# Attention and Mish block on one core: reciprocals of the first row block issued right behind kv's masks, and two weight jobs of w2 started earlier

## The chip, the cores and the metric

The kernel runs on one core of one Trainium2 chip. The core has a matrix engine (TensorE, PE in the profile, with its weight loads as PEld), a vector engine (VectorE, DVE), a scalar engine for activations (ScalarE, ACT), a general engine (GpSimd, POOL) and an engine that here only issues transfers (SyncE, SP). Each engine works through its own queue in order and waits on semaphores for the others; transfers are issued from the SP and POOL queues. The metric is the time of one execution on the device in microseconds (us). Before the change it is 505.05 us, the median of 3 runs (504.99 to 505.3).

## The reference

2,048 rows of width 512 pass through an attention part and a two-layer part, each with a layer norm, whose scale, shift and gate come from a condition vector `c`:

```python
mod = (_silu(c) @ w_mod).reshape(c.shape[0], 6, 1, -1)      # sa, ca, ga, sb, cb, gb
h = _layernorm(x) * (1 + ca) + sa
x = x + ga * A(h, A_wqkv, A_wo)
h = _layernorm(x) * (1 + cb) + sb
x = x + gb * B(h, B_w1, B_b1, B_w2)

# A: linear attention, 32 heads of width 16, phi(t) = where(t > 0, t + 1, exp(t)) + 1e-6
kv  = einsum("bhsd,bhse->bhde", phi(k), v)
z   = einsum("bhsd->bhd", phi(k))
num = einsum("bhqd,bhde->bhqe", phi(q), kv)
den = einsum("bhqd,bhd->bhq", phi(q), z)[..., None] + 1e-6
A   = (num / den) @ wo

# B: 512 -> 1792 -> 512
h = x @ w1 + b1
B = (h * tanh(softplus(h))) @ w2
```

## The kernel before, in words

**Tiling.** The rows are cut into 4 blocks of 512 (b = 0 to 3), each into 4 tiles of 128 (t). Matrix products keep nearly full float32 accuracy by splitting each operand into a high half, made by ACT as a copy, and a low half, made by DVE as the difference (`split`, line 71); `mm3` (line 65) then issues three matmuls, high by high, low by high and high by low (lines 67, 68, 69). Tiles of 128 x 512 in SBUF come from one pool of 101 places (`sb`), PSUM has three groups of buffers: `acc` (4), `h` (3) and `tp` (1).

**Order of work.** The program fixes the order by hand. Matmuls stand in the main flow; what follows a product on the other engines is written as a generator that is spawned and then moved on by one step at each `tick()`, in the order of spawning. So a `yield` means "the rest is issued one tick later", and each engine's queue has the order in which the ticks issue its instructions.

**Stages.** Keys and their sums come first, block by block. Then (from line 724) query units run, each giving one 128 x 512 piece of q, which ACT and DVE turn into phi(q) (lines 241 to 244). Between them stand the small products that make `kv` (line 746; two instructions of DVE, line 749, mask it to its 16 x 16 blocks) and from it m = kv @ wo (line 758). Every query unit's buffer is one of the three in `h`.

**The denominators** of a block are made by `attend(b, wait, queue)` (line 593). Its first step issues 32 small matmuls (line 598) into the buffer `tp`. Its second adds a small number (line 602), takes reciprocals (line 603), writes them to DRAM through `queue` (line 605) and reads them back as four tiles `rd`, spread over the heads' columns (line 609). After `wait` yields, counted from the end of that second step, the phi(q) tiles are multiplied by `rd` (line 617), two per tick, and split into halves `qs`. These are the operands of `o_unit(b, t)`, which makes the attention's output for one tile of rows; `o_post` (line 629) adds it to the input x, which empties the buffer. For blocks 0 to 2 `queue` is POOL, for block 3 it is SP.

**Around kv**: query unit (1,0), the early rows of w1 (`early_rows`), the first step of `attend(0, 4)`, the kv products, the masks, and then query units (1,1) to (1,3), each with a tick. The denominators' second step is issued in the tick behind unit (1,1), behind what was spawned earlier: modulation dot products (line 165) and the phi of unit (1,0).

**The output loop** (line 780) goes over units n = 4b + t for b = 1 to 3. Beside `o_unit` it transposes the normalised rows of blocks 0 and 1 for the second part (line 696), and at n = 5 spawns `attend(3, 3, sp)`. At n = 11 and 12 it spawns `w2_job(0)` and `w2_job(1)`. A `w2_job(f)` (line 499) asks for 128 rows of w2 on the SP queue (line 501), waits two ticks, multiplies them by the gate gb (line 504), one tick later makes the high half, one tick later the low half, and a tick after that issues two writes of these halves to DRAM on the POOL queue (line 510), from where later blocks reload them. Block 0 uses the halves directly in `d_unit`. The loop ends at n = 14; the last two output units stand among the first products of the second part, which uses a Strassen-like scheme with seven products (lines 836 to 860).

Of the kernel before, what the change touches and what calls it, by code (L numbers as in the profile page):

```python
# [13 lines left out]
P = 128  # L14
# [11 lines left out]
def block_kernel(ctx: ExitStack, tc: tile.TileContext, x, wqkv, wo, w1, b1t, w2, c, wmodt, out):  # L26
    nc = tc.nc
    act, dve, pool, pe, sp = nc.scalar, nc.vector, nc.gpsimd, nc.tensor, nc.sync
# [9 lines left out]
    def sb(name, dt=F32, shape=(P, 512)):  # L38

        return big.tile(list(shape), dt, tag="T", name=name, bufs=SLOTS)  # L40

    def ps(tag, name, shape=(P, 512)):
        return psp.tile(list(shape), F32, tag=tag, name=name, bufs=PBUFS[tag])
# [6 lines left out]
    def spawn(gen):  # L50
        fresh.append(gen)

    def tick():

        running.extend(fresh)
        fresh.clear()
        for g in list(running):
            if next(g, "end") == "end":
                running.remove(g)

    def run(gen):
        for _ in gen:
            pass
# [7 lines left out]
    def split(name, t, keep, key, lo_engine=dve, hi_engine=act):  # L71

        hi, lo = sb(f"{name}h", F32R, t.shape), sb(f"{name}l", F32R, t.shape)
        if hi_engine is act:
            act.activation(hi, t, AF.Copy)
        else:
            hi_engine.tensor_copy(hi, t)
        if lo_engine is dve:
            yield
        lo_engine.tensor_tensor(lo, t, f32(hi), op=ALU.subtract)  # L80
        keep[key] = hi, lo
# [4 lines left out]
    def load_x(b, j, key="x", eng=sp):  # L86
        t = xt[key, b, j] = sb(f"{key}_{b}_{j}")
        r0 = 512 * b + P * j
        eng.dma_start(t, x[r0:r0 + P, :])
# [84 lines left out]
    def ln_stats(key, b, j, t):  # L174

        for d, name, shape in (mv, "mv", [P, 4, 2]), (rs, "rs", [P, 4]), (nb, "nb", [P, 4]):
            if (key, b) not in d:
                d[key, b] = cst.tile(shape, F32, tag=name, name=f"{name}_{key}_{b}", bufs=NB)
        st6 = cst.tile([P, 6], F32, tag="st6", name=f"st6_{key}_{b}_{j}", bufs=4)
        dve.bn_stats(st6, t)  # L180
        dve.bn_aggr(mv[key, b][:, j, :], st6)

    def ln_eps(key, b, lo=0, hi=4):
        dve.tensor_scalar(rs[key, b][:, lo:hi], mv[key, b][:, lo:hi, 1], EPS, 1.0, op0=ALU.add, op1=ALU.mult)  # L184

    def ln_rstd(key, b, lo=0, hi=4):

        y = rs[key, b][:, lo:hi]
        pool.tensor_tensor(y, y, half[:, lo:hi], op=ALU.pow)  # L189

    def ln_shift(key, b, lo=0, hi=4):

        dve.scalar_tensor_tensor(nb[key, b][:, lo:hi], mv[key, b][:, lo:hi, 0], -1.0, rs[key, b][:, lo:hi],  # L193
                                 op0=ALU.mult, op1=ALU.mult)

    def ln_apply(key, b, j, t, dst, engine):
        if engine is act:
            act.activation(dst, t, AF.Identity, bias=nb[key, b][:, j:j + 1], scale=rs[key, b][:, j:j + 1])  # L198
        else:
            engine.tensor_scalar(dst, t, mv[key, b][:, j, 0:1], rs[key, b][:, j:j + 1],  # L200
                                 op0=ALU.subtract, op1=ALU.mult)

    def act_sums(key, b, t, v):

        if (key, b) not in rs:
            for d, name in (rs, "rs"), (nb, "nb"):
                d[key, b] = cst.tile([P, 4], F32, tag=name, name=f"{name}_{key}_{b}", bufs=NB)
        scrap = sb(f"scrap_{key}_{b}_{t}")
        sums = cst.tile([P, 2], F32, tag="sums", name=f"sums_{key}_{b}_{t}", bufs=6)
        act.activation(scrap, v, AF.Identity, scale=-1.0 / D, accum_out=sums[:, 0:1])  # L210
        act.activation(scrap, v, AF.Square, bias=sums[:, 0:1], accum_out=sums[:, 1:2])
        return sums

    def sums_eps(key, b, t, sums):
        dve.tensor_scalar(rs[key, b][:, t:t + 1], sums[:, 1:2], 1.0 / D, EPS, op0=ALU.mult, op1=ALU.add)  # L215
        ln_rstd(key, b, t, t + 1)

    def sums_shift(key, b, t, sums):
        dve.tensor_tensor(nb[key, b][:, t:t + 1], sums[:, 0:1], rs[key, b][:, t:t + 1], op=ALU.mult)  # L219
# [64 lines left out]
    def q_unit(b, g):  # L284
        p = ps("h", f"pq_{b}_{g}")
        gs = slice(P * g, P * (g + 1))
        for k in range(4):
            mm3(p, [w[:, gs] for w in wq[k]], hT["x", b, k], k == 0, k == 3)
        pq[b, g] = sb(f"q_{b}_{g}")
        spawn(phi(p, f"q_{b}_{g}", pq[b, g]))  # L290
# [205 lines left out]

    w2s, w2d, op_a = {}, {}, {}

    def w2_job(f, wait=2):
        t = sb(f"w2r_{f}")  # L500
        sp.dma_start(t, w2[P * f:P * (f + 1), :])
        for _ in range(wait):
            yield
        dve.tensor_tensor(t, t, bc["gb"], op=ALU.mult)
        yield
        yield from split(f"w2_{f}", t, w2s, f)
        yield
        for i in range(2):
            w2d[f, i] = drp.tile([P, D], F32R, name=f"w2d_{f}_{i}")
            pool.dma_start(w2d[f, i], w2s[f][i])  # L510
# [82 lines left out]
    def attend(b, wait, queue=pool):  # L593

        p = ps("tp", f"den_{b}")[:, 0:P]
        for g in range(4):
            for t in range(4):
                pe.matmul(p[32 * t:32 * (t + 1), :], hmask[:, g, :], pq[b, g][:, P * t:P * (t + 1)],
                          start=g == 0, stop=g == 3)
        yield  # L600
        rden = cst.tile([P, P], F32, tag="rden", name=f"rden_{b}", bufs=2)
        dve.tensor_scalar(rden, p, TINY, 1.0, op0=ALU.add, op1=ALU.mult)
        dve.reciprocal(rden, rden)  # L603
        d = drp.tile([32, 512], F32, name=f"rden_d_{b}")
        queue.dma_start(bass.AP(tensor=d.tensor, offset=d.offset, ap=[[P, 4], [512, 32], [1, P]]), rden)  # L605
        rd = []
        for g in range(4):
            r = sb(f"rd_{b}_{g}")
            queue.dma_start(r, bass.AP(tensor=d.tensor, offset=d.offset + 8 * g * 512,
                                     ap=[[512, 8], [0, 16], [1, 512]]))  # L610
            rd.append(r)
        for _ in range(wait):
            yield
        parts = []
        for g in range(4):
            t = pq[b, g]
            dve.tensor_tensor(t, t, rd[g], op=ALU.mult)  # L617
            parts.append(split(f"qs_{b}_{g}", t, qs, (b, g)))
            next(parts[-1])
            if g % 2:  # L620
                yield
                run(parts.pop(0))
                run(parts.pop(0))
# [32 lines left out]
    def norm_each(b, t):  # L656

        if t < 2:
            yield
            sums = act_sums("n", b, t, xt["r", b, t])  # L660
            yield
            sums_eps("n", b, t, sums)
            yield
            sums_shift("n", b, t, sums)
        else:
            ln_stats("n", b, t, xt["r", b, t])
            ln_eps("n", b, t, t + 1)
            ln_rstd("n", b, t, t + 1)
            yield
            ln_shift("n", b, t, t + 1)  # L670
        v = xt["n", b, t] = sb(f"n_{b}_{t}")
        ln_apply("n", b, t, xt["r", b, t], v, act)
# [62 lines left out]
    tick()  # L735
    run(early_rows[0])
    next(early_rows[1])
    attending = attend(0, 4)
    next(attending)
    spawn(attending)  # L740
    kv_ps = ps("acc", "kv_ps")
    for g in range(4):
        for k in range(4):
# [3 lines left out]
    for j in range(2):  # L747
        js = slice(64 * j, 64 * (j + 1))
        dve.tensor_tensor(kv.rearrange("p (g m) -> p g m", g=4)[js, :, js],
                          kv_ps.rearrange("p (g m) -> p g m", g=4)[js, :, js],  # L750
                          bmask[js, js].unsqueeze(1).to_broadcast([64, 4, 64]), op=ALU.mult)
    for g in range(1, 4):
        q_unit(1, g)
        load_x(2, g, "r")
        tick()
# [24 lines left out]
    for b in range(1, NB):  # L780
        for t in range(4):
            n = 4 * b + t
            for i, j in order.get(n, ()):
                transpose_f(i, j, "h")
                spawn(split_b(i, j, f"b{j // 2 + 1}{i + 1}"))
            if n in (12, 13):
                spawn(columns(0, n - 12, ("b11", "b12", "b21", "b22")))
            if n == 14:
                break
            o_unit(b, t)  # L790
            if b == 1:
                spawn(norm_each(1, t))
            if n == 5:
                spawn(attend(3, 3, sp))
            if n in (11, 12):
                spawn(w2_job(n - 11))
            tick()


# [185 lines left out]
```

## Time and profile before

| | us |
|---|---|
| median of 3 runs | 505.05 |
| the profiled execution, as a whole | 506.47 |
| its span, from its first to its last instruction | 504.7 |
| PE busy in the span | 495.5 |
| DVE busy | 360.3 |
| ACT busy | 257.8 |
| POOL busy | 112.9 |
| PE clock granted | 1.00 of full speed |

A row of a timeline has the start in us from the span's start, the length in us, the engine, the line of the program, the operation, the tile written, the tiles read, their shapes and a count; in brackets stands how long the engine had been idle before it and what ended that idle time. Successive rows of one engine can overlap, since an instruction starts while the one before it drains; the distance from start to start is what an instruction costs its queue. A row of the chain of waits has a start, a length and what filled it; the chain is followed back from the last instruction, at each step to what released it. In a row by windows each engine's busy time stands with its number of instructions, and behind them the granted clock, the busy share of the 16 transfer engines and the GB/s that they moved.

### The profile page before, as it was taken

Reading aid. Unit: us, or ns where it says so; the run is one execution under the profiler, and the core shown is the slowest. Engines: PE = TensorE matmul, PEld = TensorE weight load, DVE = VectorE, ACT = ScalarE, POOL = GpSimd, SP = SyncE. Lnnn points to the kernel's source line nnn. Section 1 sums busy time; section 2 is a strip of 40 time slices with the busy share of each in tenths; the row PEclk is TensorE's granted clock in tenths of the full one; section 3 lists DMA queues with packets and bytes.
Section 4 is the critical chain, followed back from the end, with each engine's and each line's share of the span. In section 5 each row is a group of like instructions: output and inputs, shape, how many; then the busy total and the mean of one; then the engine's idle time right before and its main releaser. Section 6 shows DMA issues by size and latency. Waiting matters only on the chain.

```text
span 504.7 us, 6900 instructions
## 1 busy us (share of the span) xinstructions
PE 495.5 (98%) x2396; PEld 404.9 (80%) x2396; DVE 360.3 (71%) x707; ACT 257.8 (51%) x463; POOL 112.9 (22%) x204
## 2 busy tenths in 40 slices
PE   7999999999999999999999999999999999999996
PEld 5778888878778888878888888888888888888885
DVE  6889785889987978986987785359886556745302
ACT  6767573523351987836677765357253344445000
POOL 3480000100212311210233345421210111470000
PEclk9999999999999999999999999999999999999999
DMA  8821503472553315372565499982842445597002
GB/s 282 303 83 44 166 21 105 153 244 72 137 111 92 88 33 161 125 228 66 157 197 188 145 297 260 348 240 87 249 130 59 125 126 155 157 338 236 32 1 83
DMA packets 52233, 77.29 MB, mean 153 GB/s; under 512 B 5805, under 2 KB 20277, under 8 KB 52198
## 3 DMA queue, kind: packets, MB, share of 16 engines
q0 software_dynamic: 19600, 37.45, 25.6%
q1 hardware_dynamic: 32452, 39.14, 24.6%
q8 instruction: 19, 0.31, 0.2%
q10 hardware_dynamic: 146, 0.26, 0.1%
q14 instruction: 16, 0.13, 0.1%
HBM read 60.83 MB, written 15.99 MB: 152 GB/s over the span
## 4 chain that ended last, share of the span: by engine, by line
PE 84%; DVE 9%; DMA 4%; issue 1%; ACT 1%; POOL 1%; DVEq 0%; POOLq 0%; ACTq 0%
PE oacc L69 10%; PE oacc L67 10%; PE oacc L68 10%; PE p_s L67 5%; PE p_s L69 5%; PE p_s L68 5%; PE p_a L67 3%; PE p_a L69 3%; PE p_a L68 3%; DMA rd<-rden_d 3%; PE gacc L68 3%; PE gacc L69 3%; PE gacc L67 3%; PE pk L69 2%; PE pk L68 2%; PE pk L67 2%
## 5 line engine op out<-in xcount | busy, mean ns | idle before, releaser
L516 POOL DMA_DIRECT2D w2b<-w2d x84 | 44.9, 538 | 102.3 <-PE p_a L69 27.0
L827 ACT ACTIVATE ub<-c,b1c 128x512 f32<-128x512 f32 x28 | 19.0, 718 | 57.5 <-DVE c L836 53.8
L836 DVE TENSOR_TENSOR u<-p_s,u 128x512 f32<-128x512 f32 x28 | 19.4, 692 | 35.2 <-PE p_s L69 25.5
L819 DVE TENSOR_TENSOR rb<-oacc,rb 128x512 f32<-128x512 f32 x8 | 5.5, 692 | 32.9 <-PE oacc L69 32.9
L836 DVE TENSOR_TENSOR u<-p_a,u 128x512 f32<-128x512 f32 x26 | 17.6, 689 | 7.5 <-PE p_a L69 6.9
L698 ACT ACTIVATE hf_n<-tp_n,mc 128x512 f32<-128x512 f32 x16 | 11.7, 771 | 19.5 <-PE tp_n L696 19.5
L189 POOL TENSOR_TENSOR rs_n<-rs_n,half 128x1 f32<-128x1 f32 x16 | 9.4, 589 | 53.9 <-DVE rs_n L215 44.3
L804 ACT ACTIVATE u<-u,b1c 128x512 f32<-128x512 f32 x26 | 18.5, 712 | 2.6 <-DVE u L836 2.6
L836 DVE TENSOR_TENSOR c<-p_s,u 128x512 f32<-128x512 f32 x28 | 18.0, 683 | 1.9 <-PE p_s L69 1.3
L241 ACT ACTIVATE e_q<-pq 128x512 f32<-128x512 f32 x16 | 9.3, 588 | 18.4 <-PE pq L69 18.4
L853 ACT ACTIVATE u<-p_a 128x512 f32<-128x512 f32 x12 | 7.1, 588 | 18.7 <-PE p_a L69 18.7
L241 ACT ACTIVATE e_k<-pk 128x512 f32<-128x512 f32 x16 | 9.4, 591 | 13.3 <-PE pk L69 13.1
L617 DVE TENSOR_TENSOR q<-q,rd 128x512 f32<-128x512 f32 x16 | 10.7, 689 | 6.9 <-DMA rd<-rden_d 6.8
L189 POOL TENSOR_TENSOR rs_x<-rs_x,half 128x1 f32<-128x1 f32 (+1 forms) x10 | 7.1, 716 | 32.1 <-DVE rs_x L184 31.3
L243 DVE TENSOR_SCALAR e_k<-e_k 128x512 f32<-128x512 f32 x16 | 6.9, 430 | 10.0 <-ACT e_k L241 9.9
L198 ACT ACTIVATE x<-x,nb_x,rs_x 128x512 f32<-128x512 f32 x15 | 11.6, 808 | 4.7 <-DVE nb_x L193 3.5
L605 POOL DMA_DIRECT2D rden_d<-rden x3 | 2.2, 738 | 45.7 <-DVE rden L603 45.7
L198 ACT ACTIVATE r<-r,nb_n,rs_n 128x512 f32<-128x512 f32 x8 | 6.5, 809 | 10.1 <-DVE nb_n L219 9.3
L244 DVE SCALAR_TENSOR_TENSOR q<-pq,e_q 128x512 f32<-128x512 f32 x16 | 11.1, 692 | 0.7
L244 DVE SCALAR_TENSOR_TENSOR ku<-pk,e_k 128x512 f32<-128x512 f32 x16 | 11.1, 692 | 0.7
L629 DVE TENSOR_TENSOR r<-o,r 128x512 f32<-128x512 f32 x16 | 10.8, 680 | 0.4 <-PE o L69 0.4
L180 DVE BATCH_NORM_STATS2 st_x<-x 128x6 f32<-128x512 f32 x13 | 8.9, 682 | 2.9 <-DMA x<-in_x_dram 2.9
(1118 smaller groups left out, 1751.9 us busy)
## 6 DMA issues: line engine op xcount, KB each, us to landing
w2b<-w2d POOLq DMA_DIRECT2D x84, 256.0 KB, 5.1
w1p<-in_w_dram SPq DMA_DIRECT2D x28, 256.0 KB, 3.1
wm<-in_wmodt_dram SPq DMA_DIRECT2D x24, 256.0 KB, 5.7
r<-in_x_dram SPq DMA_DIRECT2D x16, 256.0 KB, 2.4
x<-in_x_dram SPq DMA_DIRECT2D x15, 256.0 KB, 5.5
w2r<-in_w_dram SPq DMA_DIRECT2D x14, 256.0 KB, 3.4
rd<-rden_d POOLq DMA_DIRECT2D x12, 256.0 KB, 5.7
wr<-in_wqkv_dram SPq DMA_DIRECT2D x8, 256.0 KB, 3.2
```

The source lines that it names most:

```text
L67: pe.matmul(o, st[0], mv[0], start=start, stop=False)
L68: pe.matmul(o, st[0], mv[1], start=False, stop=False)
L69: pe.matmul(o, st[1], mv[0], start=False, stop=stop)
L189: pool.tensor_tensor(y, y, half[:, lo:hi], op=ALU.pow)
L198: act.activation(dst, t, AF.Identity, bias=nb[key, b][:, j:j + 1], scale=rs[key, b][:, j:j + 1])
L241: act.activation(e, p, AF.Exp)
L244: dve.scalar_tensor_tensor(dst, p, 0.0, e, op0=ALU.max, op1=ALU.add)
L516: pool.dma_start(w2s[f][i], w2d[f, i])
L698: act.activation(hf[b, j], p, AF.Identity, bias=mc[:, 12 + j:13 + j], scale=mc[:, 16 + j:17 + j])
L804: act.activation(u, p, AF.Mish, bias=b1c[:, f:f + 1])
L827: act.activation(u, p, AF.Mish, bias=b1c[:, f:f + 1])
L836: dve.tensor_tensor(out, p, u, op=ALU.add)
```

## The change

Two places are touched.

First, around kv. The generator for block 0's denominators is now advanced by hand through its second step directly behind the two masks of kv, and only then spawned. Since this step ends at the first of its waiting yields, one of them is used up at that place, and `wait` is 5 in place of 4.

Second, the first two jobs of w2. Asking for the rows becomes a function of its own, `load_w2`, which is called for f = 0 and 1 at n = 4; `w2_job` then finds them asked for and starts with the multiplication, without waiting. Both jobs are spawned at n = 7 instead of n = 11 and 12. The other twelve jobs are as before.

```diff
+    w2r = {}
+
+    def load_w2(f):
+        w2r[f] = sb(f"w2r_{f}")
+        sp.dma_start(w2r[f], w2[P * f:P * (f + 1), :])
+
     def w2_job(f, wait=2):
-        t = sb(f"w2r_{f}")
-        sp.dma_start(t, w2[P * f:P * (f + 1), :])
-        for _ in range(wait):
-            yield
+        if f not in w2r:
+            load_w2(f)
+            for _ in range(wait):
+                yield
+        t = w2r[f]
         dve.tensor_tensor(t, t, bc["gb"], op=ALU.mult)
...
-    attending = attend(0, 4)
+    attending = attend(0, 5)
     next(attending)
-    spawn(attending)
     kv_ps = ps("acc", "kv_ps")
...
                           bmask[js, js].unsqueeze(1).to_broadcast([64, 4, 64]), op=ALU.mult)
+    next(attending)
+    spawn(attending)
     for g in range(1, 4):
...
+            if n == 4:
+                load_w2(0)
+                load_w2(1)
             if n == 5:
                 spawn(attend(3, 3, sp))
-            if n in (11, 12):
-                spawn(w2_job(n - 11))
+            if n == 7:
+                spawn(w2_job(0))
+                spawn(w2_job(1))
             tick()
```

## The prediction

> **What bounds the kernel now.** I read the page first (shares, chain of waits), then the list of PE's waits, then TensorE's timeline around each wait, and last the chain that leads into it.
>
> ```profile
> span 504.7 us, 6900 instructions
> ...
> PE 495.5 (98%) x2396; PEld 404.9 (80%) x2396; DVE 360.3 (71%) x707; ACT 257.8 (51%) x463; POOL 112.9 (22%) x204
> ...
> PE 84%; DVE 9%; DMA 4%; issue 1%; ACT 1%; POOL 1%; DVEq 0%; POOLq 0%; ACTq 0%
> ```
>
> TensorE (PE) is busy 98% of the span, so only the few places where it stands still can be won. PE's own list of waits from 105 to 240 us (waiter, releaser, us in all, times, longest) has two entries:
>
> ```profile
> PE p_s L67 <- DVE r L629: 0.7, 1, 0.7
> PE o L69 <- DVE qs_2l L80: 0.4, 1, 0.4
> ```
>
> The timeline (start, length, engine, line) shows a third, shorter one, and prices them from start to start:
>
> ```profile
> 145.45 0.39 PE L69 MATMUL pq<-hT_x_3h,wq_3l 128*128 128x512 f32 x1
> 145.98 0.50 PE L67 MATMUL pq<-hT_x_0h,wq_0h 128*128 128x512 f32 x1
> 146.32 0.40 PE L68 MATMUL pq<-hT_x_0l,wq_0h 128*128 128x512 f32 x1
> ...
> 150.19 0.39 PE L67 MATMUL o<-m_2h,qs_2h 128*128 128x512 f32 x1
> 150.42 0.39 PE L68 MATMUL o<-m_2l,qs_2h 128*128 128x512 f32 x1
> 151.25 0.50 PE L69 MATMUL o<-m_2h,qs_2l 128*128 128x512 f32 x1 [0.44 <-DVE qs_2l L80]
> 151.59 0.39 PE L67 MATMUL o<-m_3h,qs_3h 128*128 128x512 f32 x1
> ...
> 218.12 0.39 PE L69 MATMUL p_s<-t_1h,s_0l 128*128 128x512 f32 x1
> 219.23 0.50 PE L67 MATMUL p_s<-t_0h,s_0h 128*128 128x512 f32 x1 [0.73 <-DVE r L629]
> 219.57 0.39 PE L68 MATMUL p_s<-t_0l,s_0h 128*128 128x512 f32 x1
> ```
>
> The undisturbed step is 0.23 (150.19 to 150.42). **Stall 1** (last query unit of block 2, waiting for a PSUM buffer): 145.98 - 145.45 - 0.23 = 0.30, and the step after it is 0.34, 0.11 more than usual: 0.41. **Stall 2** (first output unit, waiting for qs_2l): 0.83 - 0.23 = 0.60, plus 0.11: 0.71. **Stall 3** (third Strassen product, waiting for the buffer of output unit (3,0), which DVE empties late): 1.11 - 0.23 = 0.88, plus 0.11: 0.99. Together 2.11 us, all that this change can win directly.
>
> **Part A: the reciprocals of block 0.** Rows of DVE, POOL and PE, in order of time:
>
> ```profile
> 125.62 0.69 DVE L165 SCALAR_TENSOR_TENSOR wm<-wm,sc_row 128x512 f32<-128x512 f32 x1
> ...
> 127.30 0.69 DVE L244 SCALAR_TENSOR_TENSOR q<-pq,e_q 128x512 f32<-128x512 f32 x1
> ...
> 127.91 0.28 DVE L602 TENSOR_SCALAR rden<-den 128x128 f32<-128x128 f32 x1
> ...
> 128.23 0.95 DVE L603 RECIPROCAL rden<-rden 128x128 f32<-128x128 f32 x1
> ...
> 129.47 0.76 POOL L605 DMA_DIRECT2D rden_d<-rden  x1 [36.25 <-DVE rden L603]
> ...
> 129.97 0.39 PE L67 MATMUL pq<-hT_x_0h,wq_0h 128*128 128x512 f32 x1
> ...
> 132.70 2.38 POOL L609 DMA_DIRECT2D rd<-rden_d  x4 [2.48 <-PE pq L69]
> ...
> 140.68 0.69 DVE L617 TENSOR_TENSOR q<-q,rd 128x512 f32<-128x512 f32 x1 [2.12 <-DMA rd<-rden_d]
> 141.71 0.69 DVE L617 TENSOR_TENSOR q<-q,rd 128x512 f32<-128x512 f32 x1 [0.34 <-DMA rd<-rden_d]
> ...
> 145.24 0.69 DVE L244 SCALAR_TENSOR_TENSOR q<-pq,e_q 128x512 f32<-128x512 f32 x1
> ...
> 150.57 0.63 DVE L80 TENSOR_TENSOR qs_2l<-q,qs_2h 128x512 fp32r<-128x512 f32 x1
> ```
>
> No instruction is added. L602 and L603 move to where the first modulation dot product stands, right behind the masks: 127.91 - 125.62 = 2.29 us earlier. The write to DRAM and the four row reads follow them in POOL's queue, which had idled 36.25 us, so they move by 2.29 too. The count of yields goes from 4 to 5 because one is used up before the spawn; the products (L617) stay in their tick, so only their wait for data shrinks: 140.68 becomes 138.39, 141.71 becomes 139.42.
>
> What is pushed back: the two instructions (0.28 + 0.95 = 1.23 us) go ahead of two modulations and of the phi of query unit (1,0), whose last instruction ends 1.23 later, at 129.22. It frees the buffer for the unit that PE begins at 129.97; 0.75 us are left, so this costs nothing (if the cover were gone, at most 1.23 on PE). From 129.2 on DVE's queue is as before.
>
> What follows the products on DVE runs back to back up to qs_2l, so it comes earlier by what the products gain. Stall 1 was released by the instruction at 145.24: now 142.95, done 143.64, wanted at 145.68. Stall 2 by qs_2l: 150.57 + 0.63 - 2.29 = 148.91, wanted at 150.65 - 0.41 = 150.24. Both vanish as soon as the rows land 0.95 us earlier. The bounds for that landing are 0 (the transfer engines finish everything at the old time; 8 us passed between the first request and the first product) and above 2.29 (the requests now go out before SP's loads of that moment, not after). I take 2.29, since both steps behind the reciprocals waited for nothing but their predecessor. **Part A: -1.12**, between 0 and -1.12.
>
> **Part B: the rows of w2's first two jobs.** Rows of SP, of the chain of waits (start, length), of DVE, PE and ACT, and one window (the last three numbers: granted clock, share of the 16 transfer engines, GB/s):
>
> ```profile
> 183.09 0.69 SPq L605 DMA_DIRECT2D rden_d<-rden  x1
> ...
> 188.60 0.82 SPq L501 DMA_DIRECT2D w2r<-in_w_dram  x2
> ```
>
> ```profile
> 187.86 8.04 DMA rd<-rden_d
> ...
> 204.55 0.60 DVE w2r L504
> ...
> 210.67 0.69 DVE w2r L504
> ...
> 212.56 0.60 DVE w_0l L80
> ...
> 216.17 0.60 DVE w_1l L80
> ...
> 218.58 0.61 DVE r L629
> ```
>
> ```profile
> 189.74 0.69 DVE L617 TENSOR_TENSOR q<-q,rd 128x512 f32<-128x512 f32 x1 [0.56 <-DMA rd<-rden_d]
> 191.49 0.69 DVE L617 TENSOR_TENSOR q<-q,rd 128x512 f32<-128x512 f32 x1 [1.06 <-DMA rd<-rden_d]
> ...
> 197.73 0.68 DVE L80 TENSOR_TENSOR qs_2l<-q,qs_2h 128x512 fp32r<-128x512 f32 x1
> ```
>
> ```profile
> 200.62 0.39 PE L69 MATMUL o<-m_2h,qs_2l 128*128 128x512 f32 x1
> ```
>
> ```profile
> 192.22 0.63 ACT L75 ACTIVATE qs_1h<-q 128x512 fp32r<-128x512 f32 x1 [0.83 <-DVE q L617]
> ```
>
> ```profile
> 192.00:194.00 2.00, 2.00 (x13) 1.70 (x12) 2.00 (x5) 1.78 (x4) 0.00 (x0) 1.00 1.02 226
> ```
>
> Loads: two requests (0.82 us of SP) move from behind block 3's row reads to before its reciprocals' write. SP's next work is that write at 183.09, so they pass no one who is ready; and 2 x 256 KB no longer share the engines with the row reads that end the chain at 195.90 (187.86 + 8.04). A late tile buffer would hold that write; the before kernel bounds this only loosely, as w2r went out at 188.60, before its own unit.
>
> DVE: four instructions of about 0.60 each, 2.40 us, leave the unbroken DVE run that ends with the release of stall 3 at 218.58. The two multiplications land in unit 7, just ahead of the idle 0.56 and 1.06 that these rows show: nearly free. The two low halves land in unit 9, after the first two row products: 1.20 us that now stand ahead of qs_2l. So the run's end comes 2.40 - 1.20 = 1.20 earlier if the rows land as before, 2.40 or more if they land 1.2 earlier. It needs 0.88. qs_2l of block 3 ends at 198.41 + 1.20 = 199.61 at worst and is wanted at 200.62.
>
> ACT: the two high halves (0.63 each by the like row) move into a time where ACT waits 0.83 for DVE. POOL: four writes of 256 KB to DRAM move from the products behind the loop to unit 10; what reads them is a reload for the next block of rows. Part A moves PE, and with it the denominators of block 3, by 1.12 as a whole, so these leads stay. **Part B: -0.99**, between +3.4 (the slower rival) and -0.99.
>
> **Sum.** -1.12 - 0.99 = -2.11. The profiled execution took 506.47 (its span 504.7 and 1.77 around it): 504.36. The median of the runs lies 1.42 below that execution, so 505.05 - 2.11 = **502.94 us**. About 0.2%, 1.0 us here, is what a measurement tells from no change.
>
> **Rivals.**
>
> *Part B alone* (504.06): the rows of block 0 land no earlier. For it: 8 us from request to use is long, and most of it is other traffic. Against it: the requests get ahead of part of that traffic, and 0.95 of 2.29 is enough.
>
> *Part A alone* (505.05 - 1.12 = 503.93): DVE's run keeps its end, because qs_3's rows land later by as much as the run lost. For it: a margin of only 1.20 - 0.88 = 0.32 without an earlier landing. Against it: the two loads are out of their way.
>
> *Slower*: the four w2 writes leave in unit 10, beside block 3's row reads. At 226 GB/s their 1.05 MB take 4.6 us. If all of it goes ahead of the last rows, qs_2l ends at 198.41 - 1.12 + 1.20 + 4.6 = 203.1 against 199.50 on the new clock: PE waits 3.6 + 0.11. DVE's run then ends at 219.19 - 1.12 - 1.20 + 4.6 = 221.5, PE wants it at 218.35 - 1.12 + 3.7 = 220.9, so about 0.6 + 0.1 of stall 3 is left. Net: -1.12 + 3.7 - 0.99 + 0.7 = +2.3, so 507.3. It decides from 2.3 us of lateness. For it: the window's transfer share is 1.02, full. Against it: only the high halves can be ready by 190; the low halves are made at 192 or later, so half of it (2.3 us) is the natural size, and the loads taken out are as large.
>
> The Trainium skill speaks for this rival: "DMA: Bandwidth & Descriptors", section "Issuing engines are not separate DMA queues", says that transfers begun by different engines share the same 16 DMA engines and interleave. By that, giving the writes to POOL and the reads to SP separates nothing, and the time would be this rival's; the trace agrees as to sharing (the 8.04 us of the last row read, with SP's and POOL's transfers in flight).
>
> *The stalls only change place* (505.05): ACT or DVE, now fed earlier, becomes what PE waits for elsewhere. For it: DVE is busy for all of 192 to 194. Against it: the list has no further wait of PE in this stretch.
>
> **How the numbers follow.** Full forecast 0.64; part A alone 0.10; part B alone 0.08; no change 0.08; slower 0.10. Faster by over 0.2% (below 504.04): 0.64 + 0.10 = 0.74. Same: 0.08 + 0.08 = 0.16. Slower: 0.10. Range 502.4 to 504.3: the full case with 0.5 below it for the uncertain restart steps and a run's spread, and both half cases, 0.82 together.
>
> **What would show it.** L603 of block 0 at about 126 and the first row product before 139; PE steps of 0.23 through the last query unit of block 2 and the first output unit; w2r requests before 183; the last row product of block 3 no later than 194.8 (195.9 - 1.1); no PE wait for r at the third Strassen product. Wrong: the product of block 0 still near 140.7, qs_2l of block 3 behind its matmul, or a new DMA wait of a DVE instruction around 192 to 198.

## The result and the profile after

| | before | after |
|---|---|---|
| median of 16 runs each (us) | 505.58 | 504.39 |
| lowest to highest | 504.98 to 506.95 | 504.05 to 504.67 |
| ratio after / before, 95% interval | | 0.9973 (0.9966 to 0.9981) |
| the profiled execution | 506.47 | 504.41 |
| its span | 504.7 | 502.7 |

The kernel became faster by 0.27%, 1.36 us of 505.58 by the ratio, between 0.96 and 1.72 by its interval; the two medians differ by 1.19. The two profiled executions differ by 2.06. Which of the two is the effect is the question of this study.

The page of the kernel after, its first lines:

```profile
span 502.7 us, 6896 instructions
...
PE 495.2 (99%) x2396; PEld 405.5 (81%) x2396; DVE 360.1 (72%) x707; ACT 257.9 (51%) x463; POOL 113.7 (23%) x204
```

TensorE's timeline after, at the three places where it stood still before:

```profile
145.59 0.39 PE L69 MATMUL pq<-hT_x_3h,wq_3l 128*128 128x512 f32 x1
145.82 0.39 PE L67 MATMUL pq<-hT_x_0h,wq_0h 128*128 128x512 f32 x1
...
150.13 0.39 PE L68 MATMUL o<-m_2l,qs_2h 128*128 128x512 f32 x1
150.35 0.39 PE L69 MATMUL o<-m_2h,qs_2l 128*128 128x512 f32 x1
...
217.09 0.39 PE L69 MATMUL p_s<-t_1h,s_0l 128*128 128x512 f32 x1
217.32 0.39 PE L67 MATMUL p_s<-t_0h,s_0h 128*128 128x512 f32 x1
```

Each step is 0.23 or 0.22: the three waits are gone, and nothing took their place. PE has the same busy time within 0.3 us, in a span that is 2.0 shorter.

The kv part in the timeline of DVE and POOL after (lines 609 and 610 are the former 602 and 603, 616 and 624 the former 609 and 617):

```profile
125.76 0.29 DVE L609 TENSOR_SCALAR rden<-den 128x128 f32<-128x128 f32 x1
126.08 0.95 DVE L610 RECIPROCAL rden<-rden 128x128 f32<-128x128 f32 x1
...
128.58 0.69 DVE L244 SCALAR_TENSOR_TENSOR q<-pq,e_q 128x512 f32<-128x512 f32 x1
...
130.60 2.39 POOL L616 DMA_DIRECT2D rd<-rden_d  x4 [2.52 <-PE pq L69]
...
138.61 1.28 DVE L624 TENSOR_TENSOR q<-q,rd 128x512 f32<-128x512 f32 x2
...
148.33 0.63 DVE L80 TENSOR_TENSOR qs_2l<-q,qs_2h 128x512 fp32r<-128x512 f32 x1
```

Block 0's row products no longer wait for data: 138.61 has no bracket, DVE was busy until then. qs_2l is done at 148.96 for a matmul at 150.35.

The w2 part after, SP, POOL and DVE:

```profile
159.49 0.80 SPq L503 DMA_DIRECT2D w2r<-in_w_dram  x2
...
181.51 0.69 SPq L612 DMA_DIRECT2D rden_d<-rden  x1
```

```profile
189.38 0.55 POOL L517 DMA_DIRECT2D w2d<-w_0h  x1 [0.30 <-ACT w_0h L75]
...
192.66 0.53 POOL L517 DMA_DIRECT2D w2d<-w_1l  x1
```

```profile
185.65 1.28 DVE L511 TENSOR_TENSOR w2r<-w2r,gb_bc 128x512 f32<-128x512 f32 x2
...
190.02 0.69 DVE L624 TENSOR_TENSOR q<-q,rd 128x512 f32<-128x512 f32 x1 [1.19 <-DMA rd<-rden_d]
190.63 0.68 DVE L80 TENSOR_TENSOR w_0l<-w2r,w_0h 128x512 fp32r<-128x512 f32 x1
191.23 0.68 DVE L80 TENSOR_TENSOR w_1l<-w2r,w_1h 128x512 fp32r<-128x512 f32 x1
...
194.84 1.28 DVE L624 TENSOR_TENSOR q<-q,rd 128x512 f32<-128x512 f32 x2
...
215.83 1.28 DVE L636 TENSOR_TENSOR r<-o,r 128x512 f32<-128x512 f32 x2
```

The two requests for w2's rows stand 22 us ahead of the write they were meant to precede. The multiplications sit ahead of a wait, the low halves between row products. The instruction that releases the third Strassen product, the first of the two at 215.83, is done at 216.52 for a matmul at 217.32, where it held this matmul up by 0.88 before.

### The profile page after: what moved, and what is told of

Same layout as the page of the kernel before. It is cut to its first block, busy times and chain, and to the rows that moved or that the text cites. A ratio compares the mean times of both kernels' runs of the same rounds, so it can differ in the third digit from the quotient of the medians.

```text
span 502.7 us, 6896 instructions
## 1 busy us (share of the span) xinstructions
PE 495.2 (99%) x2396; PEld 405.5 (81%) x2396; DVE 360.1 (72%) x707; ACT 257.9 (51%) x463; POOL 113.7 (23%) x204
## 4 chain that ended last, share of the span: by engine, by line
PE 95%; DVE 2%; DMA 1%; ACT 1%; POOL 0%; issue 0%; ACTq 0%
PE oacc L67 10%; PE oacc L68 10%; PE oacc L69 10%; PE p_s L67 5%; PE p_s L68 5%; PE p_s L69 5%; PE p_a L67 4%; PE p_a L68 4%; PE p_a L69 4%; PE o L67 3%; PE pq L67 3%; PE o L69 3%; PE o L68 3%; PE pq L69 3%; PE pq L68 3%; PE gacc L68 3%
```

## The experiments

Theory M says that the three stalls are the whole effect and that their size differs from run to run. The rivals: what is won at kv is given back later (R), the loads and not DVE's instructions make stall 3 (L), runs differ for reasons outside these places (S). The first four kernels ran together, beside 35 runs of the kernel before (median 505.85), the next four beside 23 (median 505.76).

**1. The reciprocals alone**

```diff
-    attending = attend(0, 4)
+    attending = attend(0, 5)
     next(attending)
-    spawn(attending)
...
+    next(attending)
+    spawn(attending)
     for g in range(1, 4):
```

> Only the part at kv; w2's two jobs as before. Theory M (the three stalls of PE are the whole effect, and their size differs from run to run): stalls 1 and 2 are gone from PE's timeline, the denominators' rows are multiplied at 138.6 or so, stall 3 stays at 0.3 to 1.0 us; the time ends between that of the changed kernel (504.4) and that of before (505.6), about 504.9. Rival R (what is won at kv is given back later, as the DVE run behind block 3's rows keeps its end): stall 3 grows by what stalls 1 and 2 lost, about 2 us in its place, and the time is that of before within 0.3 us.

Median 504.82, ratio 0.9981 (0.9971 to 0.9992). Its trace has one wait of PE left, the one at the third Strassen product:

```profile
217.95 0.50 PE L67 MATMUL p_s<-t_0h,s_0h 128*128 128x512 f32 x1 [0.51 <-DVE r L629]
```

PE's steps at the places of stalls 1 and 2 are 0.23 in this trace; stall 3 is 0.77 with its slow first step, no larger than before: M, not R.

**2. The w2 part alone**: the changed kernel with the kv part put back to `attend(0, 4)`, its second step in the tick.

> Only w2's part; the reciprocals at kv as before. M: stalls 1 and 2 stay (0.4 to 1.2 us together), stall 3 is gone; the time is about 505.0. R (this part alone does the whole work): 504.4, with no wait of PE at 219 and none at 146 and 151.

Median 505.20 (lowest to highest 504.30 to 506.17), ratio 0.9978 (0.9967 to 0.9990). DVE and PE in its profiled execution, which took 506.17:

```profile
141.84 1.29 DVE L624 TENSOR_TENSOR q<-q,rd 128x512 f32<-128x512 f32 x2 [3.35 <-DMA rd<-rden_d]
```

```profile
146.72 0.50 PE L67 MATMUL pq<-hT_x_0h,wq_0h 128*128 128x512 f32 x1 [0.94 <-DVE q L244]
...
151.98 0.50 PE L69 MATMUL o<-m_2h,qs_2l 128*128 128x512 f32 x1 [0.42 <-DVE qs_2l L80]
```

Stalls 1 and 2 stay, 1.90 us here, and stall 3 is gone. The size is above the expectation's upper end of 1.2: DVE waited 3.35 for the rows, where it had waited 2.12 in the first trace of before.

**3. The loads early, the jobs late**

```diff
-            if n == 7:
+            if n == 13:
                 spawn(w2_job(0))
-                spawn(w2_job(1))
             tick()
+
+    spawn(w2_job(1))
```

> The changed kernel, but the two w2 jobs multiply and split at their old places; only their loads are early. If DVE's four instructions make stall 3 (theory of the prediction): a wait of 0.3 to 0.9 us is back at the third Strassen product, time 504.6 to 505.2. If it is the loads, which share the transfer engines with block 3's rows (rival L): no wait there, time 504.4, and the last row product of block 3 comes at 194 or earlier.

Median 504.80, ratio 0.9974 (0.9964 to 0.9984). Its trace:

```profile
217.52 0.50 PE L67 MATMUL p_s<-t_0h,s_0h 128*128 128x512 f32 x1 [0.16 <-DVE r L636]
```

Stall 3 is back, 0.43 us with its slow first step, as the prediction's theory has it. The median is within 0.02 that of the reciprocals alone (504.82), and 0.41 above that of the changed kernel, so asking for w2's rows early brings nothing that these medians can tell. The ratios alone would not decide it: 0.9974 here and 0.9973 for the whole change, beside runs of before that lie anywhere from 504.6 to 508.3. What decides is the trace. DVE on the way to the release, here and in the kernel after:

```profile
210.16 0.69 DVE L848 TENSOR_TENSOR c<-p_a,u 128x512 f32<-128x512 f32 x1 [0.46 <-ACT u L853]
...
216.78 1.29 DVE L636 TENSOR_TENSOR r<-o,r 128x512 f32<-128x512 f32 x2
```

```profile
210.41 0.69 DVE L848 TENSOR_TENSOR c<-p_a,u 128x512 f32<-128x512 f32 x1
...
215.83 1.28 DVE L636 TENSOR_TENSOR r<-o,r 128x512 f32<-128x512 f32 x2
```

In experiment 3 DVE had caught up and waited for ACT at line 848, so the rows no longer set the time there. From this addition to the release are 6.62 us, after the change 5.42: the difference of 1.20 is the two low halves, which stand in between in experiment 3 and not after. So L falls as the cause of this stall.

In the traces 4 and 7 the same addition (line 836 of the kernel before) also starts a little late, 0.82 and 0.67 after the instruction ahead of it, where 0.60 is DVE's usual distance; in these two and in 3, stall 3 is 0.42 or 0.43; where DVE goes into this addition without a break (the first trace of before, 1, 5, 8), it is 0.53 to 1.30, and the release follows the second row product of block 3 by 26.79 to 27.05. By these traces stall 3 has a part of some 0.43 that the low halves make, and a part that comes and goes with the landing of block 3's rows. Whether the early loads make that landing earlier isn't shown.

**4. The kernel before, once more** (no edit to the program)

> The kernel before, run once more for its trace and as its own comparison: ratio 1.000 within 0.1%. M: the time of its profiled execution less the stalls read from its PE timeline is 504.4 within 0.2 us, and its stalls are below 2.11 us if that time is below 506.47. Rival S (runs differ for a reason that lies outside these three places, such as the start or the end): the stalls are 2.1 us again, whatever the time.

Ratio 0.9999 (0.9986 to 1.0012). Its profiled execution took 505.24:

```profile
140.49 1.30 DVE L617 TENSOR_TENSOR q<-q,rd 128x512 f32<-128x512 f32 x2 [1.90 <-DMA rd<-rden_d]
```

```profile
150.63 0.50 PE L69 MATMUL o<-m_2h,qs_2l 128*128 128x512 f32 x1 [0.23 <-DVE qs_2l L80]
...
218.06 0.50 PE L67 MATMUL p_s<-t_0h,s_0h 128*128 128x512 f32 x1 [0.15 <-DVE r L629]
```

Stall 1 is absent, stall 2 is 0.50, stall 3 is 0.42: 0.92 in place of 2.11, in the same program.

**5. Less traffic beside block 0's rows** (from the kernel before)

```diff
     for g in range(4):
         q_unit(2, g)
...
-        load_x(3, g, "r")
         tick()
...
         q_unit(3, g)
+        load_x(3, g, "r")
         tick()
```

> The kernel before, with block 3's four loads of x asked for among block 3's query units instead of block 2's; the reciprocals stay late. If the late landing of block 0's rows comes from transfers that share the engines with them (T): the first row product comes at 139.8 or earlier (140.5 to 141.8 in the traces of kernels with late reciprocals), stalls 1 and 2 shrink to 0.3 us or less together, time 504.8 to 505.2. If the landing takes its 8 us by itself (rival): the product stays at 140.5 to 141.8, stalls 1 and 2 at 0.5 to 1.8, time 505.4 to 505.9.

Median 506.17, ratio 1.0013 (0.9999 to 1.0028). The first row product, with the reciprocals as late as before, and the place where PE waits now:

```profile
138.33 1.28 DVE L617 TENSOR_TENSOR q<-q,rd 128x512 f32<-128x512 f32 x2
...
159.28 0.69 DVE L617 TENSOR_TENSOR q<-q,rd 128x512 f32<-128x512 f32 x1 [1.74 <-DMA rd<-rden_d]
```

```profile
218.58 0.50 PE L67 MATMUL p_s<-t_0h,s_0h 128*128 128x512 f32 x1 [1.04 <-DVE r L629]
```

The first half of T, that other transfers delay the rows, holds in this trace: the rows were there when DVE asked, and stalls 1 and 2 are gone without touching the reciprocals. The time does not follow (forecast 504.8 to 505.2). SP now asks for the four moved loads at 146.86 to 153.17. Block 1's first two row products wait 4.00 us together, against 2.04 to 2.79 in the nine other traces, and stall 3 is 1.30 in this trace. That the moved loads cause the longer wait and the larger stall is argued, not shown.

**6. The jobs at unit 5**

```diff
-            if n == 7:
+            if n == 5:
                 spawn(w2_job(0))
                 spawn(w2_job(1))
```

> The changed kernel with w2's two jobs spawned at unit 5, so that their four writes are issued two units earlier, at about 185 to 188, together with the requests for block 3's rows. Slower rival of the prediction (the writes go ahead of the rows): the last row products come 2 us or more later than 194.8, PE waits up to 2 us at output unit (3,0), time 504.8 to 506.5. Theory M (the rows have room): they come up to 2 us later, but PE does not wait before the third Strassen product, and the time is 504.4 within 0.3.

Median 504.34 (lowest to highest 504.10 to 504.60), ratio 0.9967 (0.9954 to 0.9980). The four writes and the row products that were to suffer:

```profile
186.99 0.62 POOL L517 DMA_DIRECT2D w2d<-w_0h  x1
...
188.68 0.54 POOL L517 DMA_DIRECT2D w2d<-w_1l  x1
```

```profile
189.42 0.69 DVE L624 TENSOR_TENSOR q<-q,rd 128x512 f32<-128x512 f32 x1 [0.70 <-DMA rd<-rden_d]
...
193.03 1.28 DVE L624 TENSOR_TENSOR q<-q,rd 128x512 f32<-128x512 f32 x2
```

With all four writes asked for before the wait for rows ended, the products come at 189.42 and 193.03, earlier than after (190.02 and 194.84). The writes didn't speed them up: most of the difference is that the two low halves, 1.20 us between these products after, are made at 183.32 here. The fair comparison is experiment 3, whose writes go out only from 208.65 on: 189.31 and 192.92. PE has no wait. The slower rival falls; the times of this kernel and of the changed one overlap, so it isn't shown to be better.

**7 and 8. The kernel before, two more traces** (no edit to the program)

> The kernel before, one more trace. M: own time less the stalls in its PE timeline is 504.3 within 0.2 us, with stalls of another size than 2.11 and 0.92. Rival S: stalls and time are unrelated.

> As the one before: own time less stalls 504.3 within 0.2 us.

They took 508.02 and 505.05. The longer one, DVE and then PE, and below them the shorter one:

```profile
143.24 1.29 DVE L617 TENSOR_TENSOR q<-q,rd 128x512 f32<-128x512 f32 x2 [4.10 <-DMA rd<-rden_d]
```

```profile
148.12 0.50 PE L67 MATMUL pq<-hT_x_0h,wq_0h 128*128 128x512 f32 x1 [1.70 <-DVE q L244]
...
153.38 0.50 PE L69 MATMUL o<-m_2h,qs_2l 128*128 128x512 f32 x1 [0.44 <-DVE qs_2l L80]
```

```profile
139.60 1.29 DVE L617 TENSOR_TENSOR q<-q,rd 128x512 f32<-128x512 f32 x2 [0.80 <-DMA rd<-rden_d]
```

In the shorter one DVE still waited 0.80 for the rows but PE not at all: stalls 1 and 2 can be absent in the unchanged kernel.

**All traces together.** Stalls are read from PE's timeline from start to start, with 0.11 for the slower step behind each wait, as in the prediction:

| trace | its time | stalls 1 and 2 | stall 3 | time less stalls |
|---|---|---|---|---|
| before (the one predicted from) | 506.47 | 1.12 | 0.99 | 504.36 |
| before, 4 | 505.24 | 0.50 | 0.42 | 504.32 |
| before, 7 | 508.02 | 2.67 | 0.43 | 504.92 |
| before, 8 | 505.05 | 0 | 0.53 | 504.52 |
| reciprocals alone, 1 | 505.17 | 0 | 0.77 | 504.40 |
| w2 part alone, 2 | 506.17 | 1.90 | 0 | 504.27 |
| loads early, 3 | 504.75 | 0 | 0.43 | 504.32 |
| after | 504.41 | 0 | 0 | 504.41 |
| jobs at unit 5, 6 | 504.34 | 0 | 0 | 504.34 |

Times from 504.34 to 508.02 come down to one floor between 504.27 and 504.52, but for one trace. The traces 7 and 8 miss what was expected of them, 504.3 within 0.2: the first by 0.42, the second by 0.02. In trace 7, PE reached block 0's denominators at 121.93, 0.44 later than after (121.49), so most of its extra lies ahead of the three places. Experiment 5 has a further short gap of 0.33 and lands at 504.19. Counted from the start of these denominators on PE, which lies between 121.21 and 121.93, the time less stalls is 382.88 to 383.01 in all ten traces. So the stalls make nearly all of the difference between these traces, and S keeps only a rest of up to 0.7 us, which arises ahead of the denominators and whose cause stays open.

## Why the prediction was right in its mechanism and too large in its size

**The three stalls, their causes and their end**: right. All three are gone, each by the route that was forecast. The reciprocals moved as worked out (1.23 us pushed onto the phi of query unit (1,0), done at 129.27 against a forecast of 129.22, without a wait of PE). The first row product came at 138.61 (forecast 138.39), where DVE's own queue and no longer the data sets the time, and experiment 1 shows part A alone doing this. The forecast of 2.29 for the landing itself was too small for at least one of the four reads, which did no harm: from request to landing the fastest of the four reads took 6.4 to 9.7 us in the four traces of before, and 4.2 to 4.4 in the four traces with the early reciprocals (1, 3, 6 and after). So one of the reads at least had landed by 132.4 + 4.4 = 136.8 after the change, where in the first trace of before none had by 140.6.

**"As soon as the rows land 0.95 us earlier"**: borne out by the traces of before. At 140.68 and 140.49 the first row product leaves stalls, at 139.60 none.

**Part B**: right as to what releases stall 3. The releasing instruction starts 2.66 earlier (218.49 to 215.83); 1.12 of this is part A's, and the 1.54 left lies between the two bounds of 1.20 and 2.40. The loads were counted at nothing for their move; the medians of experiments 1 and 3 agree. The low halves did stand ahead of qs_2l, and had room: it is done at 197.93 for a matmul at 199.60. One of the prediction's own signs was missed here. The last row product of block 3 was to come no later than 194.8 and came at 195.44, the second of the two at 194.84, because these low halves stand ahead of it; PE doesn't notice.

**The rivals**: part A alone and part B alone are what experiments 1 and 2 made by hand, and neither half swallowed the other's. The stalls did not change place. The slower rival had sharing for it, and experiment 6 gave it a better chance than the change did; the rows came no later.

**The step that failed** is the term of the sum in "The median of the runs lies 1.42 below that execution, so 505.05 - 2.11 = 502.94". The 2.11 us were measured in an execution of 506.47, and were taken from runs that did not have them. 506.47 is 1.42 above the median just because its stalls were larger than usual. The subtraction has to stay inside one execution: 506.47 - 2.11 = 504.36, which the changed kernel's median (504.39) meets within 0.03. Against runs of 505.05 that is a gain of 0.69, against the 16 runs' median of 505.58 it is 1.22; the medians differ by 1.19. The first three runs happened to be among the quick ones: of the 16, only two lie below 505.05. By the medians of the two halves, the usual stalls 1 and 2 are 505.20 - 504.39 = 0.81 and the usual stall 3 is 504.82 - 504.39 = 0.43, where the profiled execution had 1.12 and 0.99.

That the stated range of 502.4 to 504.3 came so close is in part luck. The time of 504.39 lies just above it; the gain of 1.36 taken off 505.05 gives 503.69 and lies inside. But the range reached so far up for the two half cases (503.93 and 504.06), and neither of these happened.

The sign was in front of the reader: the profiled execution lay above the highest of the three runs (505.3), and all three stalls stand behind a transfer, stalls 1 and 2 behind block 0's rows and stall 3, by the prediction's own chain of waits, behind block 3's.

## What to carry to other kernels

A stall that hangs on a transfer had no single size here: stalls 1 and 2 together came to anything from 0 to 2.67 us in one program. Take such a stall off the execution in which it was measured, and what is left is the floor of the kernel without it; the gain is the distance from the usual run to that floor, not the stall of the one execution. Where a profiled execution lies above the usual runs, look first whether its waits for transfers make the difference. And when such a stall is removed with room to spare, expect the spread to shrink too: here from 1.97 us over 16 runs to 0.62.

## What the runs showed of the hardware

The same four row reads, 256 KB each, asked for by the same instruction, took very different times. From the first request to the first row product it was 140.68 - 132.70 = 7.98 us in the first trace of before, 7.74 in experiment 4, 9.94 in 7 and 6.64 in 8; with the program unchanged, the last two decide whether PE stalls by 2.67 us or not at all. What makes them differ isn't shown. In experiment 5 it was at most 138.33 - 132.58 = 5.75; of the four x loads that it moves, two had been asked for beside these reads (at 131.71 and 132.66 in the first trace of before) and two some 8 us earlier. The Trainium skill says in "DMA: Bandwidth & Descriptors", section "Issuing engines are not separate DMA queues", that transfers begun by different engines run on the same 16 engines and interleave; the one trace of experiment 5 agrees for reads beside reads. Experiment 6 shows that sharing need not cost the transfer that is waited for: 1 MB of writes beside the rows of block 3 held the row product that waits for them up by no more than 0.11 (189.42 against 189.31 in experiment 3). The writes bore it: from request to landing they took 6.7 to 7.0 us, against 2.5 to 3.7 in experiment 3, where they go out later, and PE has no wait behind them.

One side effect was not foreseen. SP's loads of that time moved too, one of x from 132.66 to 136.45; that it now waits for a place in memory, since the rows' tiles are taken earlier, is likely, not shown. This took traffic away from block 0's rows as well, in every kernel with the early reciprocals, and was not tried apart from them: how much of part A is the early request and how much the later load stays open.
